# Clamps moved from right in front of two copies, a reordered rounding and 11 fewer filler products in the opening of an attention-plus-MLP kernel

## The chip, the cores and the metric

One core of a Trainium2 chip (trn2). The metric is device microseconds of one execution; lower is better. PE is TensorE, DVE is VectorE, ACT is ScalarE, SP issues the transfers. "Mean clock" is the mean granted clock of TensorE over one execution, as a share of full speed. PSUM is the memory that the kernel's products are written to, in banks (`ps` in the code).

## The reference

```python
def _attn_ref(x, state):                      # B,H,S,Ns,D = 8,8,512,32,64
    scores = matmul(x, state.T) / sqrt(D);  a = softmax(scores);    xread = matmul(a, state)
    scores2 = matmul(state, x.T) / sqrt(D); a2 = softmax(scores2);  sread = matmul(a2, x)
    return concatenate([xread, sread], axis=2)
def _moe_ref(x, w_in, w_out):                 # 4352 tokens, 512 -> 2048 -> 512
    h = x @ w_in
    g = h * (1 / (1 + exp(-1.702 * h)))
    return (g @ w_out).astype(float32)
```

(Shortened to its arithmetic.) The weights arrive as 64-bit floats. They are read as pairs of 32-bit words and rounded to fp32 on the chip: that is the "rounding" of this document. There are 16 pieces of w_in (128 x 512 each, numbered from 0) and 16 of w_out.

## The kernel before

The kernel multiplies state and w_in first: M(b, c) is batch b's state times column block c of w_in, and needs pieces 4c to 4c+3. The up-projection `up_x(b, f)` then multiplies M by the attention weights aT(b). Every M leaves PSUM through a ScalarE copy, and every up-projection block through a gelu on ScalarE. Rounding a piece takes one VectorE mask (it cuts the exponent bits out), two ScalarE clamps (they keep the exponent in range) and four VectorE steps. Batch 0's four blocks go by while batch 1's attention weights are being normalised on VectorE (`att_x_norm`).

```python
def round_a(i):
    ...
    # the two clamps of a piece of w_in, the second reads the first's result
    nc.scalar.activation(out=sc.bitcast(FP32), in_=sc, func=AF.Relu, bias=edge[0], scale=-8.0)     # L200
    nc.scalar.activation(out=sc, in_=sc.bitcast(FP32), func=AF.Relu, bias=edge[1], scale=-1.0)     # L201

def round_b(i):
    ...
    nc.vector.tensor_scalar(fr, hi, 0xFFFFF, 0x100000, ALU.bitwise_and, ALU.bitwise_or)            # L210 fraction
    nc.vector.scalar_tensor_tensor(sc, hi, -0x80000000, sc, ALU.bitwise_and, ALU.bitwise_or)       # L211 sign
    nc.vector.scalar_tensor_tensor(dst, lo, 2.0**-32, fr, ALU.mult, ALU.add)                       # L212 sum
    nc.vector.scalar_tensor_tensor(dst, dst, 2.0**-20, sc.bitcast(FP32), ALU.mult, ALU.mult)       # L213 product

def att_M(b, c, spare=False):
    ps = [psH.tile(...) if spare else att_ps(...) for g in range(NG)]
    by_state(b, ps, lambda rows, j: w_in[c][rows, j])         # quarter j reads piece 4c+j
    for g in range(NG):
        nc.scalar.copy(m[:, g], ps[g])                        # L418

# the opening, from batch 1's scores on
att_scores(1)
keep_warm(14)                 # products of zeros
powers_to(4)
round_to(NPR, 2)              # piece 3; masks and clamps two pieces ahead
att_M(0, 0)
att_blocks(1); att_x_exp(1)
up_x(0, 0); up_x(0, 1); up_x(0, 2, True); up_x(0, 3, True)
round_to(NPR + 1)             # piece 4, with masks and clamps of pieces 6 and 7
att_x_norm(1)
att_M(1, 0)
turn(1, 0, None, [1, 1])      # four up_x(1, .), a rounding after each of the first two
round_to(2 * NPR)             # piece 7, with the clamps of piece 10
att_M(0, 1)
turn(0, 1, (1, 1), [1, 1, 1])
...
```

## Time and profile before

| | before |
|---|---|
| median of the first 3 runs | 744.18 us (743.77 to 744.27) |
| span of the profiled run, mean clock | 742.8 us, 0.998 |
| PE busy | 728.4 us, 98% |
| PE still between M(1,0) and its first product | 2.12 us |
| PE still between M(0,1) and its first product | 1.50 us |

The page's busy shares and the chain are shown in the prediction. The timeline of PE says the same from PE's side; columns are start us, length us, engine, line, operation, output and inputs, count, and in brackets how long the engine stood still before it and who ended that:

```profile
38.01 1.84 PE L289 MATMUL M<-w_in,stT 64*32 64x512 f32 x16
41.97 7.13 PE L458 MATMUL h<-low,M 128*128 128x512 f32 x16 [2.12 <-ACT M L418]
49.04 1.09 PE L289 MATMUL M<-w_in,stT 64*32 64x512 f32 x16
51.63 5.42 PE L458 MATMUL h<-aT,M 128*128 128x512 f32 x12 [1.50 <-ACT M L418]
```

M(1,0) takes 1.84 us instead of 1.09: its second bank is freed only by the newest gelu, which ends at 38.72, and the other products start at 38.77. Then PE stands still twice for a ScalarE copy.

### The profile page before, as it was taken

What the parts mean: (1) busy time and instruction counts of PE and PEld (TensorE: products, weight loads), DVE (VectorE), ACT (ScalarE), POOL (GpSimd) and SP (SyncE); (2) the same over time, 40 slices, a digit from 0 to 9 for tenths busy, and PEclk for the clock granted to TensorE, in tenths of its full rate; (3) what the DMA queues carried; (4) which work ended last, traced back from release to release, by engine and by line L of the source; (5) the groups of instructions that cost most, each with busy time, mean ns of one, the idle gap of its engine ahead of it and who ended that gap; (6) DMA issues with size and microseconds to landing.
All of it is one profiled execution on the core that took longest, in us unless ns stands there. A gap on an engine that the chain in (4) does not pass through costs nothing.

```text
span 742.8 us, 11102 instructions
## 1 busy us (share of the span) xinstructions
PE 728.4 (98%) x4624; PEld 567.7 (76%) x4626; DVE 510.9 (69%) x982; ACT 232.4 (31%) x424; POOL 0.8 (0%) x8
## 2 busy tenths in 40 slices
PE   8989999999999999999999999999999999999996
PEld 3423454467898788888888789878987988899995
DVE  6999799819856776567747776687566774767340
ACT  4676611024214511533133422451143313300220
POOL 0000000000000000000000000000000000000000
PEclk9999999999999999999999999999999999999999
DMA  8921246010031000300040004000130001000000
GB/s 221 351 67 50 84 155 161 0 44 15 15 86 19 1 15 29 75 1 15 1 103 1 15 1 99 6 8 8 36 69 1 15 10 35 1 15 30 15 1 28
DMA packets 48770, 35.31 MB, mean 48 GB/s; under 512 B 36432, under 2 KB 44112, under 8 KB 48720
## 3 DMA queue, kind: packets, MB, share of 16 engines
q1 hardware_dynamic: 48720, 34.61, 16.3%
q8 instruction: 36, 0.59, 0.3%
q14 instruction: 14, 0.11, 0.0%
HBM read 25.69 MB, written 8.91 MB: 47 GB/s over the span
## 4 chain that ended last, share of the span: by engine, by line
PE 96%; DMA 2%; ACT 1%; SPq 0%; issue 0%; DVE 0%; DVEq 0%; ACTq 0%
PE o L642 33%; PE o L887 16%; PE h L458 8%; PE o L476 7%; PE low L594 7%; PE upx L887 6%; PE o L594 5%; PE M L289 4%; PE o L519 2%; PE xT L268 2%; PE warm L122 1%; PE o L289 1%; PE sr L438 1%; PE upx_sr L887 1%; DMA out_dram<-osb_sr 1%; PE eT L427 1%
## 5 line engine op out<-in xcount | busy, mean ns | idle before, releaser
L642 PE MATMUL o<-w_out,g 128*128 128x256 f32 x672 | 151.8, 380 | 0.0
L897 DVE TENSOR_TENSOR g<-o,g 128x512 f32<-128x512 f32 (+1 forms) x140 | 88.1, 651 | 88.4 <-PE o L887 87.4
L642 PEld LDWEIGHTS o<-w_out,g 128*128 128x128 f32 x672 | 125.2, 190 | 21.7 <-issue 5.5
L894 ACT ACTIVATE g<-g 128x512 f32<-128x512 f32 (+1 forms) x84 | 49.8, 599 | 100.5 <-DVE g L897 100.5
L642 PE MATMUL o<-sums,g 128*128 128x256 f32 x224 | 51.1, 382 | 0.0
L642 PE MATMUL o<-sums,later 128*128 128x256 f32 x224 | 49.5, 379 | 0.0
L887 PE MATMUL upx<-aT,M 128*128 128x256 f32 x192 | 49.3, 379 | 0.0
L642 PEld LDWEIGHTS o<-sums,g 128*128 128x128 f32 x224 | 41.5, 190 | 10.1 <-issue 5.0
L887 PE MATMUL o<-ta,M 128*128 128x256 f32 x192 | 49.3, 379 | 0.0
L887 PE MATMUL o<-ta,ms 128*128 128x256 f32 x192 | 48.3, 379 | 0.0
L642 PEld LDWEIGHTS o<-sums,later 128*128 128x128 f32 x224 | 42.6, 190 | 5.8
L418 ACT COPY M<-M 128x512 f32<-128x512 f32 x64 | 33.2, 596 | 38.7 <-PE M L289 38.7
L887 PEld LDWEIGHTS o<-ta,ms 128*128 128x128 f32 x192 | 36.5, 190 | 5.0
L887 PEld LDWEIGHTS upx<-aT,M 128*128 128x128 f32 x192 | 36.5, 190 | 5.0
L887 PEld LDWEIGHTS o<-ta,M 128*128 128x128 f32 x192 | 36.5, 190 | 5.0
L597 DVE TENSOR_TENSOR pu<-low,pu 128x128 f32<-128x128 f32 x14 | 4.1, 290 | 43.5 <-PE low L594 43.5
L499 DVE TENSOR_TENSOR later<-g,g 128x512 f32<-128x512 f32 (+1 forms) x32 | 20.8, 650 | 19.1 <-ACT g L461 19.1
L289 PE MATMUL M<-w_in,stT 64*32 64x512 f32 x512 | 33.2, 594 | 0.2 <-ACT eT L428 0.2
L458 PE MATMUL h<-low,M 128*128 128x512 f32 x64 | 29.8, 600 | 2.1 <-ACT M L418 2.1
L458 PE MATMUL h<-aT,M 128*128 128x512 f32 x64 | 28.7, 599 | 2.3 <-ACT M L418 2.3
L476 PE MATMUL o<-w_out,g 128*128 128x512 f32 x64 | 28.7, 594 | 0.0
L476 PE MATMUL o<-w_out,sums 128*128 128x512 f32 x64 | 28.4, 594 | 0.0
(176 smaller groups left out, 1102.6 us busy)
## 6 DMA issues: line engine op xcount, KB each, us to landing
later<-in_moe_w_out_dram SPq DMA_DIRECT2D x16, 512.0 KB
xn<-in_x_dram SPq DMA_DIRECT2D x28, 256.0 KB
w_out<-in_moe_w_in_dram SPq DMA_DIRECT2D x12, 512.0 KB
out_dram<-osb SPq DMA_DIRECT2D x18, 256.0 KB
out_dram<-later SPq DMA_DIRECT2D x14, 256.0 KB
later<-in_moe_w_in_dram SPq DMA_DIRECT2D x4, 512.0 KB
sums<-in_x_dram SPq DMA_DIRECT2D x4, 256.0 KB
stn<-in_state_dram SPq DMA_DIRECT2D x16, 32.0 KB
```

The lines of the kernel that those rows point to most:

```text
L268: nc.tensor.transpose(ps[:, c], x_heads(b, c, j), ident)
L289: nc.tensor.matmul(ps[g][st], A[b]["stT"][rows, st], rhs(rows, j), start=True, stop=True)
L418: nc.scalar.copy(m[:, g], ps[g])
L458: nc.tensor.matmul(hps, lhs[i], rhs[i], start=(i == 0), stop=(i == n - 1))
L476: nc.tensor.matmul(ops, G[key, f // 2][:, f % 2, P * r : P * (r + 1)], w_out[:, f], start=(f == 0), stop=(f == NF - 1))
L499: nc.vector.tensor_tensor(out=s1, in0=a21, in1=a22, op=ALU.add)
L519: nc.tensor.matmul(ps[:, r], lhs[f][:, P * r : P * (r + 1)], rhs[:, f], start=(first and r == 0 and f == 0), stop=(f == HF - 1), skip_grou ...
L594: nc.tensor.matmul(ps, lhs[f], rhs[:, f], start=(f == 0), stop=(f == QF - 1))
L642: nc.tensor.matmul(ps[:, r], lhs[f][:, P * r : P * (r + 1)], rhs[:, f], start=(r == 0 and f == 0), stop=(f == HF - 1), skip_group_check=True,)
L887: nc.tensor.matmul(ps[:, k], lhs[i][:, o : o + P], rhs[i], start=(first and k == 0 and i == 0), stop=(i == n - 1), skip_group_check=True,)
L894: nc.scalar.activation(out=dst, in_=src, func=AF.Gelu_apprx_sigmoid)
L897: nc.vector.tensor_tensor(out=dst, in0=ps, in1=x, op=ALU.add)
```

## The change

Its intent: let nothing but gelus stand right in front of the copies of M(1,0) and M(0,1) on ScalarE's queue, give M(1,0) banks that are free already, put another step between a rounding step and the one that uses its result where there is one to put, and issue 3 products of zeros where 14 were. The clamps of pieces 6 and 7 move behind the copy of M(1,0). Those of piece 10 stay ahead of the copy of M(0,1), but move from behind the fourth gelu of M(1,0) to before it.

```diff
-    def round_b(i):
+    def fraction(i):
...
+        nc.vector.tensor_scalar(dst.bitcast(I32), words(i)[1], 0xFFFFF, 0x100000, ALU.bitwise_and, ALU.bitwise_or)
+        begun[i] = dst
+    def round_b(i, ahead, follows):
...
+        if i not in begun:
+            fraction(i)
...
-        nc.vector.tensor_scalar(fr, hi, 0xFFFFF, 0x100000, ALU.bitwise_and, ALU.bitwise_or)
         nc.vector.scalar_tensor_tensor(sc, hi, -0x80000000, sc, ALU.bitwise_and, ALU.bitwise_or)
-        nc.vector.scalar_tensor_tensor(dst, lo, 2.0**-32, fr, ALU.mult, ALU.add)
+        powers_to(ahead)
+        nc.vector.scalar_tensor_tensor(dst, lo, 2.0**-32, dst.bitcast(I32), ALU.mult, ALU.add)
...
+        if follows and i + 1 in raw:
+            fraction(i + 1)
         nc.vector.scalar_tensor_tensor(dst, dst, 2.0**-20, sc.bitcast(FP32), ALU.mult, ALU.mult)
...
+    powers_to(1)
+    fraction(0)
     powers_to(2)
     round_to(2, 0)
...
-    keep_warm(14)
+    keep_warm(3)
     powers_to(4)
-    round_to(NPR, 2)
+    round_to(NPR, 1)
     att_M(0, 0)
+    powers_to(NPR + 2)
...
+    att_M(1, 0, True)
     round_to(NPR + 1)
     att_x_norm(1)
-    att_M(1, 0)
...
-    turn(1, 0, None, [1, 1])
-    round_to(2 * NPR)
+    turn(1, 0, None, [1, 1, 1])
     att_M(0, 1)
```

More of the change, by code (lines that the diff above doesn't have):

```diff
@@ L148 @@
     PIECES = [("i", c, k) for c in range(NFC) for k in range(NPR)] + [("o", f) for f in range(NF)]
-    raw, power = {}, {}
+    raw, power, begun = {}, {}, {}
     AHEAD = 3
@@ L201, in round_a @@
         nc.scalar.activation(out=sc, in_=sc.bitcast(FP32), func=AF.Relu, bias=edge[1], scale=-1.0)
-    def round_b(i):
+    def fraction(i):
         key = PIECES[i]
         dst = w_in[key[1]][:, key[2]] if key[0] == "i" else w_out[:, key[1]]
-        fr = dst.bitcast(I32)
+        nc.vector.tensor_scalar(dst.bitcast(I32), words(i)[1], 0xFFFFF, 0x100000, ALU.bitwise_and, ALU.bitwise_or)
[3 more added lines that the diff above has]
+            fraction(i)
+        dst = begun.pop(i)
         lo, hi = words(i)
         sc = power.pop(i)
-        nc.vector.tensor_scalar(fr, hi, 0xFFFFF, 0x100000, ALU.bitwise_and, ALU.bitwise_or)
         nc.vector.scalar_tensor_tensor(sc, hi, -0x80000000, sc, ALU.bitwise_and, ALU.bitwise_or)
-        nc.vector.scalar_tensor_tensor(dst, lo, 2.0**-32, fr, ALU.mult, ALU.add)
+        powers_to(ahead)
+        nc.vector.scalar_tensor_tensor(dst, lo, 2.0**-32, dst.bitcast(I32), ALU.mult, ALU.add)
+        del raw[i]
+        if follows and i + 1 in raw:
+            fraction(i + 1)
         nc.vector.scalar_tensor_tensor(dst, dst, 2.0**-20, sc.bitcast(FP32), ALU.mult, ALU.mult)
-        del raw[i]
     done = {"load": 0, "a": 0, "b": 0, "credit": 0.0}
@@ L234, in round_to @@
     def round_to(n, ahead=AHEAD):
+        nin = NFC * NPR
         while done["b"] < min(n, len(PIECES)):
-            powers_to(min(done["b"] + 1 + ahead, max(NFC * NPR, done["b"] + 1)))
-            round_b(done["b"])
+            i = done["b"]
+            powers_to(i + 1)
+            round_b(i, min(i + 1 + ahead, max(nin, i + 1)), i + 1 < nin and (i + 1 < n or i >= NPR))
             done["b"] += 1
```

## The prediction

> **What bounds the kernel now.** I read the page's busy shares first, then the chain of work that ended last for 0 to 240 us, then VectorE's and ScalarE's timelines for 0 to 75 us, where the diff's lines stand.
>
> ```profile
> PE 728.4 (98%) x4624; PEld 567.7 (76%) x4626; DVE 510.9 (69%) x982; ACT 232.4 (31%) x424; POOL 0.8 (0%) x8
> ```
>
> TensorE is busy for 98% of a 742.8 us span and the chain is 96% PE. A change that adds and removes no product of the result can win only where PE runs filler (the products of zeros, "warm") or stands still. The diff touches nothing after about 75 us except the order of VectorE's work, so the whole prize lies in the first 52 us. The chain of waits there (columns: start us, length us, what):
>
> ```profile
> 26.42 2.75 PE warm L122 x12
> 29.17 1.16 PE M L289 x16
> 30.33 0.57 ACT M L418
> ...
> 30.95 7.15 PE h L458 x16
> ...
> 38.12 0.60 ACT g L461
> 38.72 0.62 ACT low L200
> ...
> 39.36 0.72 ACT low L201
> 40.08 0.62 ACT low L200
> ...
> 40.73 0.72 ACT low L201
> 41.45 0.48 ACT M L418
> ...
> 41.97 7.15 PE h L458 x16
> ...
> 49.74 0.62 ACT low L200
> ...
> 50.38 0.72 ACT low L201
> 51.11 0.48 ACT M L418
> ...
> 51.63 5.42 PE h L458 x12
> ```
>
> Three things are to be seen. M(0,0) starts at 29.17, exactly where the warm products end: 14 of them fill 26.05 to 29.17, or 0.223 us each. M(1,0) goes to PE at 38.10, but its copy (line 418) starts on ScalarE only after four clamps (lines 200 and 201, those of pieces 6 and 7), and the next real product comes at 41.97. M(0,1) meets the same at 49.1: one pair of clamps (piece 10) stands ahead of its copy, and PE restarts at 51.63. From 51.63 on the chain is PE without a gap worth naming, until two copies of 0.6 us at 87 and 99.8 us that the diff leaves alone.
>
> VectorE's timeline (start, length, engine, line, operation) gives the rounding:
>
> ```profile
> 25.13 0.44 DVE L210 TENSOR_SCALAR w_in<-w_out 128x512 int32<-128x512 int32 x1
> 25.47 0.70 DVE L211 SCALAR_TENSOR_TENSOR low<-w_out,low 128x512 int32<-128x512 int32 x1
> 26.07 0.70 DVE L212 SCALAR_TENSOR_TENSOR w_in<-w_out,w_in 128x512 f32<-128x512 uint32 x1
> 26.81 0.69 DVE L213 SCALAR_TENSOR_TENSOR w_in<-w_in,low 128x512 f32<-128x512 f32 x1
> 27.41 1.31 DVE L320 STREAM_TRANSPOSE e<-o 128x512 f32<-128x512 f32 x2
> ...
> 37.21 1.25 DVE L370 STREAM_TRANSPOSE low<-e 128x1024 f32<-128x1024 f32 x1
> ```
>
> Piece 3, the last that M(0,0) needs, is done at 27.50, so even now M(0,0) waits 1.6 us for filler alone. Line 370 ends at 38.46: it writes the normalised weights of batch 1, without which the products after M(1,0) cannot start. That is a second floor close under ScalarE's.
>
> **What the Trainium skill says.** "ScalarE: Activation LUTs", section "What ACT_TABLE_LOAD costs", gives an ACTIVATE with a pointer bias as about 280 ns + 0.833 ns per column, 706 ns for 512, and says that back-to-back ones overlap by about 93 ns. The trace agrees: 706 to 716 ns for line 200, and 0.63 us from a line-201 start to the next line-200 start. Line 201 reads what line 200 wrote and starts 0.75 us after it, with no overlap. "VectorE: DVE Perf Modes", section "The DRAIN you can't avoid", says that the next operation waits until the pipe is empty. Here it depends on the data: line 212 starts 0.60 us after the 0.70 us line 211, whose result it does not use; line 213 starts 0.74 us after line 212, whose result it does use. So a use of the predecessor's result costs some 0.12 us. "TensorE: Matmul & The Clock Gate", section "Part 1: The HAM clock gate", says that an idle window of about 3.4 us halves the clock; the longest stillness of PE in this stretch is 2.12 us and the granted clock is 0.998. The change shortens those gaps, so I expect no cold product from cutting the filler.
>
> **The change part by part.** Start-to-start steps from the trace: fraction or mask 0.34 us, each three-operand step 0.61, plus 0.11 to 0.13 where a step uses its predecessor's result.
>
> *Front, to 26 us.* Rounding of pieces 0 and 1 starts 2 us earlier for one fraction and ends at about 11.5 instead of 11.95, but VectorE next waits for PE at 12.26 and PE waits for x from memory. Worth 0.
>
> *Fewer products of zeros.* In the old order a mask of piece 5 waited 0.5 us for its transfer ahead of piece 3's rounding. In the new one VectorE, free at 23.89, does fraction 23.89, sign 24.23, mask of piece 4 at 24.84, sum 25.18, product 25.91 (0.73 later, this one still uses its predecessor), done at 26.6. PE: scores end at 26.05, 3 fillers with the 0.05 issue end at 26.7 to 26.9. The two nearly tie; I take 26.8. M(0,0) moves from 29.17 to 26.8: **2.37 us**. Its copy needs ScalarE at 27.94, where the clamps of piece 4 end at about 26.7. Products of M(0,0) then start at 26.8 + 1.78 (30.95 less 29.17) = 28.58.
>
> *M(1,0)'s copy ahead of four clamps.* PE is through four blocks at 28.58 + 7.15 = 35.73 and goes to M(1,0). It now has the other pair of banks, so it need not wait for the newest gelus (in the old trace that stretches M(1,0) to 1.84 us). The copy starts at 35.73 + 1.14 = 36.87, and by it alone products could start at 37.51. But VectorE: mask of piece 5 at 26.52, blocks 26.86, maximum 28.21, subtraction 29.46, fraction 4 at 30.60, sign 30.94, two masks to 32.22, sum, fraction 5, product at 33.17, then sum of exponentials 33.78 and the same chain of 1.24 + 0.22 + 0.39 + 1.25 us to the transpose at 36.88, which ends at 38.13. Products of M(1,0) start at 38.17, VectorE setting it. From M(1,0) to there is 2.44 us instead of 3.87: **1.43 us**.
>
> *M(0,1)'s copy ahead of clamps.* ScalarE, through M(1,0)'s copies at 37.83, now does the postponed clamps of pieces 6 and 7 (2.74 us as before) until 40.57, then three units of a gelu and two clamps (0.49 + 0.75 + 0.63 = 1.86 us), the fourth gelu at 46.16, and the copy of M(0,1) at 46.65 with nothing between. Products follow 0.62 us after the copy's start, as before: 47.27. PE would be at M(0,1) at 38.17 + 7.15 = 45.32 and done at 46.34, so ScalarE is 0.3 us behind it. Start to start 9.10 instead of 9.66 us: **0.56 us**. Piece 7, by VectorE's new cycle of 2.51 us (old 2.73), is done at about 45.7; M(0,1) uses it only in its last quarter, so that fits barely.
>
> *After that.* Everything from 51.63 moves as a block to 47.27. VectorE gains less (piece 15 done at about 64.5 instead of 67.2), but M(0,3), which needs it, comes at about 69, and VectorE stands still 5.14 us for ScalarE's exponentials near 79 as it is. The shorter cycle of the later roundings is therefore worth nothing by itself there. Sum: 2.37 + 1.43 + 0.56 = 4.36 us; 744.18 - 4.36 = 739.8, or 0.6% less.
>
> **The rivals.** First, the floor under M(1,0): if VectorE's order gains nothing (dependent or not), its normalisation ends near 38.5 and the second part shrinks by 0.4, but ScalarE's backlog sets 47.27 anyway: 739.8 to 740.2. Second, clamps postponed are not removed: if ScalarE's backlog of 2.74 us runs on, gelus come late, PE waits for banks, and M(0,1) keeps its old delay: the third part becomes 0 or -1 us, 740.4 to 741.4. For it: ScalarE is solid from 37 to 47 us by my sum, its 1.86 us unit is longer than PE's 1.79 us block. Against it: it idled 1.59 and 0.86 us in the same stage before. Third, piece 3 or piece 7 late on VectorE makes PE wait where filler stood: 0.3 to 1 us lost. Fourth, the gain is given back before 83 us because VectorE's rounding or a transfer becomes the bound: 741 to 744; against it, the first product at 83.14 needs a piece finished at 73.9. Fifth, a better outcome, if normalisation ends before the copy: up to 0.6 us more at the second part, but ScalarE's backlog swallows it.
>
> **Range and chances.** The predicted time is 739.8 us. Run to run the kernel before spreads 0.5 us; the three terms are uncertain by about 0.2, 0.4 and 0.6 us, more to the slow side: 738.9 to 741.2 in 8 of 10. A gain over 2% would need 14.9 us, more than all of PE's stillness and filler in this stage after 26 us; a loss over 2% has no source. So faster 0.01, same 0.98, slower 0.01.
>
> **What would show it.** In the changed profile: M(0,0) on PE at 26.8; the first product of M(1,0) at about 38.2, released by VectorE's transpose of line 370's kind and not by a copy; the clamps of pieces 6 and 7 after the copy of M(1,0); the first product of M(0,1) at about 47.3 behind ScalarE; PE solid from there, the chain's later entries all about 4.4 us earlier. It is wrong if M(0,0) starts later than 27.2 (piece 3 is late), if PE shows a new wait for a bank between 38 and 47 us, or if the shift at the first down product (83.14 before) is less than at 47.

## The result, and the profile after

The changed kernel took 739.31 us (median of 4 runs, 739.24 to 739.40); beside it the kernel before took 744.22 us (median of 4, 743.77 to 745.60). The ratio is 0.9931, 95% interval 0.9914 to 0.9948: "same" at the 2% mark, and the gain is real. A ratio is the mean time of one kernel's runs over the mean of the other's of the same rounds, so not quite the ratio of the medians.

The chain of waits of the changed kernel (start us, length us, what; lines are shifted by 13 against before: 471 for 458, 302 for 289, 431 for 418, 474 for 461):

```profile
25.83 0.38 PE warm L122
26.21 1.16 PE M L302 x16
...
27.98 7.13 PE h L471 x16
35.11 1.13 PE M L302 x16
36.24 1.05 ACT M L431 x2
37.30 0.63 ACT low L200
...
45.59 0.48 ACT g L474
46.07 0.53 ACT M L431
...
46.65 5.42 PE h L471 x12
```

M(0,0) follows 3 fillers. The copy of M(1,0) stands directly behind M(1,0). From there the chain runs through ScalarE alone, five pairs of clamps and four gelus, to the copy of M(0,1). PE's timeline has the other two limits of the stage:

```profile
37.59 7.10 PE L471 MATMUL h<-low,M 128*128 128x512 f32 x16 [1.46 <-DVE low L383]
44.62 1.35 PE L302 MATMUL M<-w_in,stT 64*32 64x512 f32 x16
46.65 5.42 PE L471 MATMUL h<-aT,M 128*128 128x512 f32 x12 [0.67 <-ACT M L431]
```

The first product of M(1,0) waits for VectorE's last step of the normalisation (line 383), no longer for a copy. M(0,1) takes 1.35 us instead of 1.09: VectorE ends piece 7 at 44.87, and the four products that read it end 1.1 us after that. And the product behind it waits for ScalarE. Without any wait M(0,1) would have ended at 45.71; piece 7 puts that to 45.97, and ScalarE is through its gelus at 46.07. Three limits lie within 0.4 us.

| stretch, PE's view of the chain | before | after | gain |
|---|---|---|---|
| end of batch 1's scores to start of M(0,0) | 26.05 to 29.17 = 3.12 | 25.45 to 26.21 = 0.76 | 2.36 |
| to the first product of M(1,0) | 12.80 | 11.38 | 1.42 |
| to the first product of M(0,1) | 9.66 | 9.06 | 0.60 |
| to the first down-projection product | 31.51 | 31.50 | 0.01 |
| sum | | | 4.39 |

The two profiled spans differ by 742.8 - 737.6 = 5.2 us. Of the rest, 0.60 us lies ahead of all this: x arrived sooner, so the scores ended at 25.45 instead of 26.05. The experiments say what that is. The last 0.25 us lies far behind the change, where ScalarE waits for an output tile to be stored before it refills it. Before, then after:

```profile
165.64 0.58 ACT L483 COPY osb<-o 128x512 f32<-128x512 f32 x1 [3.83 <-DMA out_dram<-osb]
158.95 0.58 ACT L496 COPY osb<-o 128x512 f32<-128x512 f32 x1 [2.13 <-PE xT L281]
```

In five of the fourteen profiles (both of the kernel before, and those of a_warm14, b_order and b_copies, which are told of below) the third store of this group takes 2.48 to 2.82 us, and the one 16 KB packet of the instruction queue falls into it. In the other nine that packet falls elsewhere, the store takes 1.17 to 1.43 us, and nothing is lost. The five lose 0.2 to 0.6 us by it near 189 us. This meeting of two transfers is read from the traces; no run tests it.

### The profile page after: what moved, and what is told of

Read it like the earlier page. It is cut to its first block, busy times and chain, and to the rows that moved or that the text cites. A ratio compares the mean times of both kernels' runs of the same rounds, so it can differ in the third digit from the quotient of the medians.

```text
span 737.6 us, 11080 instructions
## 1 busy us (share of the span) xinstructions
PE 724.4 (98%) x4613; PEld 566.4 (77%) x4615; DVE 509.7 (69%) x982; ACT 232.3 (31%) x424; POOL 0.8 (0%) x8
## 4 chain that ended last, share of the span: by engine, by line
PE 95%; ACT 2%; DMA 2%; SPq 0%; DVE 0%; issue 0%; DVEq 0%; ACTq 0%
PE o L655 33%; PE o L900 16%; PE o L489 8%; PE low L607 7%; PE h L471 7%; PE upx L900 6%; PE o L607 5%; PE M L302 4%; PE o L532 2%; PE xT L281 2%; PE o L302 1%; PE sr L451 1%; PE warm L122 1%; PE upx_sr L900 1%; DMA out_dram<-osb_sr 1%; PE eT L440 1%
## 5 line engine op out<-in xcount | busy, mean ns | idle before, releaser
L614 ACT COPY pu<-o 128x128 f32<-128x128 f32 x14 | 3.7, 265 | 80.0 <-PE o L607 60.0
```

## The experiments

Kernels named a_ are the changed kernel with one thing undone, b_ the kernel before with one part alone, c_ are attempts to go further. All gave correct results. In the traces I compare the stretch from the start of M(0,0) to the first product of M(0,1): 22.46 us before, 20.44 after. It is free of the arrival of x.

### 14 fillers again

```diff
-    keep_warm(3)
+    keep_warm(14)
```

> The changed kernel with 14 products of zeros again in place of 3, all else as changed. My theory: M(0,0) starts 11 x 0.215 = 2.36 us later (about 28.6 us if the front is that of the changed profile), ScalarE's solid stretch from the copy of M(1,0) on moves with it, and the whole delay reaches the end: 739.3 + 2.3 = 741.6 us (741.2 to 742.0). Rival: VectorE, which does not move with the filler, is the real bound in the stage behind it, so that part of the delay is absorbed there: 739.3 to 740.5 us.

Measured 741.87 us (741.63 to 742.24, 4 runs), 2.56 more than the changed kernel. M(0,0) starts at 28.53 instead of 26.21, and the first product of M(0,1) at 48.92 instead of 46.65, 2.27 later. So the filler's time goes through to the end in full (the rest of the 2.56 us is the late store told of above). VectorE absorbed part of it at the first product of M(1,0), which comes 1.59 us later (39.18 instead of 37.59), but not at M(0,1), where ScalarE's queue sets the time.

### M(1,0) late again

```diff
-    att_M(1, 0, True)
     round_to(NPR + 1)
     att_x_norm(1)
+    att_M(1, 0)
```

> The changed kernel with M(1,0) put back behind the rounding of piece 4 (four clamps ahead of its copy on ScalarE, the old pair of banks). My theory: the copy starts near 38.4 us instead of 36.2, the first product of M(1,0) near 39.0 instead of 37.6, but ScalarE then has no backlog at M(0,1), so about 1.2 us reaches the end: 740.5 us (740.2 to 740.9). Rival, that postponed clamps only move the wait (the copies' place is worth nothing): 739.3 us within 0.2.

Measured 741.36 us (740.67, 740.89, 741.82, 742.57). From M(0,0) at 26.25 to the first product of M(0,1) at 47.96 are 21.71 us: 1.27 us more, as expected. The run takes back the place and the banks of M(1,0) together; none separates them. The faster two runs agree with that (1.4 to 1.6 us over the changed kernel). The slower two do not; the one at 742.57 has a mean clock of 0.997, the others 0.999 to 1.0. More on this below. PE's old 2.12 us of stillness is back:

```profile
35.09 1.84 PE L302 MATMUL M<-w_in,stT 64*32 64x512 f32 x16
39.05 7.13 PE L471 MATMUL h<-low,M 128*128 128x512 f32 x16 [2.12 <-ACT M L431]
```

### M(0,1) behind clamps again

```diff
-    turn(1, 0, None, [1, 1, 1])
+    turn(1, 0, None, [1, 1])
+    round_to(2 * NPR)
```

> The changed kernel with the clamps of piece 10 ahead of M(0,1)'s copy again. My theory: the fourth gelu then waits for PE to 44.8 us and the clamps behind it put the copy at about 46.65 instead of 46.0: + 0.65 us, 739.95 us (739.7 to 740.2). Rival, that ScalarE's backlog is the same in either order: 739.3 us.

Measured 739.94 us (739.84 to 740.12), 0.63 more; the first product of M(0,1) is at 47.34, 0.69 later with a front that is 0.1 later. As expected.

### The old order inside a rounding

The old `round_b` with its masks first, in the changed kernel's places; the front of pieces 0 and 1 as before.

> The changed kernel with the old order inside a rounding (masks first, then the four steps one after another, no fraction of the next piece in between; also the old front for pieces 0 and 1). My theory: VectorE's order is worth little; piece 7 comes some 1 us later, and M(0,1) waits for it in its last quarter: + 0.2 to 0.3 us, 739.55 us (739.3 to 739.9). Rival, that the reordering earns most of the gain: 740.8 us or more. Front: if the 0.6 us by which x arrived sooner in the changed profile was only a difference from run to run, it may be seen with this old front too; if the earlier fraction brought it, the first transpose of x is back at 9.0 us and the time near 740.1.

Measured 739.83 us (739.75 to 740.31), 0.52 more, at the upper side of what I expected. The reordering is worth half a microsecond, and here is where: M(0,1) now waits longer for piece 7.

```profile
44.38 1.96 PE L292 MATMUL M<-w_in,stT 64*32 64x512 f32 x16
```

Against 1.35 us in the changed kernel and 1.09 without any wait. VectorE ends piece 7 at 45.24 here, and M(0,1) ends at 46.34; in the changed kernel it was 44.87 and 45.97. Both times M(0,1) ends 1.10 us after its last piece. The first transpose of x stood at 8.28 us, earlier than in any profile so far, with the old front. So the earlier fraction is not what brought x sooner.

### The kernel before once more

> The kernel before, unchanged, as a control of the front. In its first profile the first transpose of x stood at 8.99 us, in the five profiles of the changed family at 8.28 to 8.54, and its time spread over 2.5 us in the last rounds (743.69 to 746.18). If that is the x transfer's difference from run to run, this profile may show another value anywhere in 8.2 to 9.5 and its times spread again (743.5 to 746.5); if something in the program makes x late, it stands at 9.0 again. From the first M product to the first product of M(0,1) I expect 22.46 us as before in either case.

Measured 744.33, 743.90, 745.58, 745.63, 744.28 and 745.76 us. In its profile the first transpose of x stood at 8.42 us (8.99 in its first profile, 8.40 in the changed kernel's), with an unchanged program. The 0.60 us at the front is therefore a difference from run to run, not part of the change. The stretch from M(0,0) at 28.57 to the first product of M(0,1) at 51.03 is 22.46 us again. (Its span is only 0.25 us shorter all the same, because it loses 0.60 us by the late store where the first profile loses 0.25.) But its times fall into two groups: three at 743.9 to 744.3 with a mean clock of 0.998, three at 745.6 to 745.8 with 0.996.

### Only the new order of a rounding

The kernel before with the new `fraction`, `round_b` and `round_to`, and the early fraction of piece 0.

> The kernel before with only the new order inside a rounding and the early fraction of piece 0; 14 fillers and the old places of the copies. My theory: M(0,0) waits for filler and the copies for clamps, so the order is worth nothing here: the stretch from M(0,0) to the first product of M(0,1) stays 22.4 us within 0.3, the time is that of the kernel before within 0.3 us (if the front is alike). Rival, that the order by itself earns much of the gain: at least 2 us less.

Measured 745.59 us (744.29 to 746.01), ratio 1.0002 (0.9988 to 1.0017): nothing by itself. Four of five runs have a mean clock of 0.996 or 0.997, and this profile fell on one of them. PE's timeline and then the clock by stretch (start:end us, length, busy time and count of each engine, granted clock, share of DMA, GB/s):

```profile
41.33 8.83 PE L471 MATMUL h<-low,M 128*128 128x512 f32 x16 [2.12 <-ACT M L431]
```

```profile
41.33:42.50 1.17, 1.17 (x3) 0.68 (x4) 1.17 (x4) 0.43 (x1) 0.00 (x0) 1.00 0.00 0
42.50:44.00 1.50, 1.50 (x3) 0.67 (x2) 1.50 (x4) 0.09 (x1) 0.00 (x0) 0.54 0.05 11
44.00:45.50 1.50, 1.50 (x3) 0.47 (x3) 0.80 (x2) 1.47 (x3) 0.00 (x0) 0.50 0.00 0
```

The same stretch of the second profile of the kernel before, a run at 0.998:

```profile
42.50:44.00 1.50, 1.50 (x4) 0.60 (x4) 1.47 (x5) 0.60 (x2) 0.00 (x0) 1.00 0.00 0
44.00:45.50 1.50, 1.50 (x5) 0.73 (x4) 1.43 (x4) 1.47 (x3) 0.00 (x0) 1.00 0.00 0
```

Sixteen products that take 7.13 us elsewhere took 8.83 here, because TensorE's clock fell to half 1.28 us after the end of the 2.12 us gap. The trace's clock record has it at 0.5 for 3.413 us. That explains the two groups of times, as far as one profile of a slow-clock run can. Take those 1.70 us off, and the stretch from M(0,0) at 28.53 to the first product of M(0,1) at 52.68, 24.15 us, is 22.45: unchanged by the order.

### Only the filler

```diff
-    keep_warm(14)
+    keep_warm(3)
```

> The kernel before with 3 products of zeros in place of 14, nothing else. My theory: M(0,0) is then held by piece 3, done 2.1 us before the point where it began before minus the mask's wait, so it starts 1.6 us sooner (27.55 with the old front), not 2.4; the stage behind moves with it because the copies wait for clamps that follow the gelus: 1.6 us less (1.3 to 1.9). Rival: VectorE's normalisation, which does not move, holds the first product of M(1,0), and 0.5 us or less is left. Second rival: fewer fillers let the clock fall, and products of the stage behind get longer than 0.43 us of PE each.

Measured 743.04 us: 741.97 and 742.07 at a clock of 0.998 and 0.999, and 743.12, 743.65 and 743.04 at 0.996 and 0.997. The profile is one of the first kind. M(0,0) starts at 26.26, at once behind the 3 fillers and not at 27.55 as I wrote: its first three quarters need only pieces 0 to 2. It then waits for piece 3 in its last quarter and lasts 1.70 us instead of 1.16. It ends at 27.96 instead of 29.73, and the first product of M(0,1) comes at 49.27 instead of 51.03: 1.76 us, close to the 1.6 expected. What this leaves of the changed kernel's 2.36 us is 0.6 us, which took moving the mask of piece 5, with its wait for a transfer, behind the rounding of piece 3: a_oldbody, with the old order inside a rounding but the new places, has M(0,0) at its full speed (1.09 us).

### Only the copies

```diff
-    round_to(NPR + 1)
-    att_x_norm(1)
-    att_M(1, 0)
+    att_M(1, 0, True)
+    round_to(NPR + 1)
+    att_x_norm(1)
...
-    turn(1, 0, None, [1, 1])
-    round_to(2 * NPR)
+    turn(1, 0, None, [1, 1, 1])
```

> The kernel before with only the two copies of M ahead of the clamps (M(1,0) in the other pair of banks), 14 fillers and the old order. My theory: from M(0,0) at 29.17 the copy of M(1,0) is at 39.2, the first product at 39.9 instead of 41.97, ScalarE's backlog sets the copy of M(0,1) at 49.0 and its first product at 49.6 instead of 51.63: 2.0 us less (1.7 to 2.3). Rival, postponed clamps give it all back: within 0.4 us of the kernel before.

Measured 741.90 us (741.77 to 742.44). From M(0,0) at 28.71 to the first product of M(0,1) at 49.10 are 20.39 us, 2.07 less than before, as expected. And none of its five runs is a slow-clock one (0.998 to 1.0).

### Filler in the gap

The new theory: PE's 2.12 us of stillness lets the clock fall in some executions. It is tested by filling the gap, in the kernel before.

```diff
     att_x_norm(1)
     att_M(1, 0)
+    keep_warm(8)
```

> The kernel before with 8 more products of zeros behind M(1,0), in the 2.12 us in which PE stands still there. New theory (from the earlier runs): some executions of every kernel with that 2.12 us gap ran about 1.7 us longer at a mean clock of 0.996 or 0.997, and the one profile of such a run shows half clock for 3.4 us right behind the gap; the gap lets the clock fall. Then the filler (8 x 0.215 = 1.7 us, fits in the gap) takes the slow executions away and costs nothing: all runs within 743.6 to 744.6 us, none at 745.4 or above, where about half of the kernel before's are. Rival: the clock's fall has nothing to do with that gap: about half of these runs again lie at 745.4 to 746.2.

Measured 743.73, 743.71, 743.77, 744.78 and 743.78 us, all at a mean clock of 0.998 or more. Of the eight runs of the kernel before in the same rounds, five were at 745.4 to 745.8 with 0.996 or 0.997. The filler hides in the gap, which is now 0.29 us, and the products behind stay where they were:

```profile
39.37 1.67 PE L122 MATMUL warm<-sums 128*128 128x512 bf16 x7 [0.16 <-issue]
41.33 1.98 PE L458 MATMUL h<-low,M 128*128 128x512 f32 x4 [0.29 <-ACT M L418]
```

The run at 744.78 lies a little outside what I expected, but its clock did not fall; it is unexplained, like the 741.82 above. Counted over all runs whose clock was listed, "slow-clock" meaning 0.996 or 0.997 and over 1 us above the kernel's fastest (the mean clock alone does not tell: every profile also ends with 2.71 to 5.70 us at half clock, after the last product):

| kernels | PE still behind M(1,0) | slow-clock runs |
|---|---|---|
| before (with its control) | 2.12 us | 14 of 22 |
| b_order, b_warm3, a_m10_late | 2.12 us | 4 of 5, 3 of 5, 1 of 4 |
| b_gapfill | 0.29 us | 0 of 5 |
| the changed kernel and all others | 0.73 to 1.46 us | 0 of 36 |

For the kernel before, the mean of the 14 is 745.66 us and of the other 8 it is 744.23: 1.4 us.

Why does the clock fall in only some executions with the same gap? The clock records of the traces show it. In all 14 traces the clock changes only at marks 3.413 us apart (the stretches at full clock last 11, 204, 214 or 215 times that), and the first mark lies anywhere from 3.90 to 7.17 us after the start. Cut each trace into windows at these marks, and sum how long PE stood still in each. The 15 windows that end in a fall (14 behind the last product, and the one of b_order) hold 2.12 us of stillness or more. The other 2986 windows at full clock hold 1.83 us or less. In the profiles with the 2.12 us gap the window with most of it holds:

| profile | PE still in one window | clock falls |
|---|---|---|
| before, before_again, a_m10_late, b_warm3 | 1.52, 1.69, 1.74, 1.83 us | no |
| b_order | 2.12 us, the whole gap | yes |

So a gap of 2.12 us matters when a window takes in nearly all of it, and by these figures one of 1.46 us does not. By my estimate from these figures a random position of the marks gives a fall in 38% to 55% of executions; 22 of 36 is 61%. No run was made to test this.

### Going further: the normalisation first

```diff
-    round_to(NPR + 1)
-    att_x_norm(1)
+    att_x_norm(1)
+    round_to(NPR + 1)
```

> The changed kernel with batch 1's normalisation on VectorE ahead of the rounding of piece 4, so that it ends near 35.5 us instead of 37.4 and the first product of M(1,0) waits only for its copy (36.85 instead of 37.6). My theory that ScalarE's backlog sets the first product of M(0,1): nothing is gained, 739.3 us within 0.2. Rival that VectorE's normalisation is the bound of the stage: 0.7 us less, 738.6 us.

Both theories missed. Measured 740.61 us (740.50 to 741.86), 1.3 us slower than the changed kernel. VectorE, put on the normalisation first, has to stand still for ScalarE's exponentials, and everything behind it, up to piece 7, comes later. VectorE's timeline shows the loss and PE's shows who pays:

```profile
31.18 1.22 DVE L378 TENSOR_REDUCE sm<-e 128x32 f32<-128x1024 f32 x1 [1.12 <-ACT e L371]
```

```profile
36.89 7.55 PE L471 MATMUL h<-low,M 128*128 128x512 f32 x16 [0.73 <-ACT M L431]
44.37 1.08 PE L302 MATMUL M<-w_in,stT 64*32 64x512 f32 x12
46.19 1.05 PE L302 MATMUL M<-w_in,stT 64*32 64x512 f32 x4 [0.74 <-DVE w_in L225]
```

The first product of M(1,0) does come 0.7 us sooner. But the last four products of M(0,1) wait for piece 7 (line 225) until 46.19. They then last 1.05 us, about as long as the twelve before them (1.08) or all sixteen together (1.09): the quarters run side by side, and a late one costs nearly the whole time of an M. So the first product of M(0,1) comes at 47.90 instead of 46.65. In the changed kernel the rounding of piece 4 fills the time in which the exponentials run.

### Going further: both, and fewer ahead

c_both also does the clamps of piece 6 ahead of the fourth gelu of M(0,0); c_best also drops the filler ahead of M(0,0) and lets masks and clamps run two pieces ahead instead of three.

```diff
     up_x(0, 2, True)
+    powers_to(NPR + 3)
     up_x(0, 3, True)
```

> As c_norm_first, and the clamps of piece 6 done ahead of the fourth gelu of M(0,0), where ScalarE idles 1.1 us. If ScalarE's backlog of four clamps and VectorE's normalisation together are the bound, the copy of M(0,1) starts at about 45.15 us (PE and piece 7 set it) instead of 46.0: 0.85 us less, 738.45 us (738.1 to 738.8). If something else holds PE there, within 0.2 us of 739.3.

> As c_both, with no filler ahead of M(0,0) (its last quarter then waits for piece 3) and masks and clamps one piece less ahead (two instead of three). M(0,0) starts at 25.5 us and ends at 26.6 instead of 27.4; piece 7 is done at 44.4 and sets M(0,1)'s last quarter; first product of M(0,1) near 45.4 instead of 46.65: 1.2 us less than the changed kernel, 738.1 us (737.7 to 738.6). If clamps come too late for VectorE with one piece less ahead, 738.5 to 739.5.

Measured 740.27 us (740.12 to 740.95) and 739.88 us (739.84 to 740.06). Both keep VectorE's wait for the exponentials of c_norm_first (0.79 us is left as stillness, a mask fills the rest) and with it the wait for piece 7: M(0,1)'s last quarter starts at 45.67 and 45.42. My expectations had worked out piece 7 for both as if VectorE lost nothing. In c_best M(0,0) starts at 24.51, but its last quarter waits for piece 3 to 25.97, so most of the filler's removal is lost too. No version beat the changed kernel.

## Why the prediction was right or wrong

The time was right: 739.8 us predicted, 739.31 measured, inside 738.9 to 741.2, and "same" at the 2% mark. The measured gain, 744.22 - 739.31 = 4.91 us, is 0.5 us above the sum of the terms, 4.36. The 8 undisturbed later runs of the kernel before (mean 744.23) say the same. The late store, 0.25 and 0.60 us in the two profiles of the kernel before and not in the changed kernel's, is of that size; the prediction did not foresee it.

*The three terms* were right one by one. Fewer products of zeros: 2.37 us predicted, 2.36 in the table of stretches. M(1,0): 1.43 and 1.42, and set by VectorE's transpose as written. M(0,1): 0.56 and 0.60, set by ScalarE. Undoing the first in the changed kernel costs 2.27 us at the first product of M(0,1); undoing the copies' places one at a time costs 1.27 and about 0.6.

*The front, worth 0,* was right. The 0.60 us by which the changed kernel's profile was ahead there comes and goes in the kernel before itself (8.99 and 8.42 us).

*After 51.63 everything moves as a block* was right: 31.51 and 31.50 us to the first down-projection product.

*The reordering worth little* was right for the kernel before (ratio 1.0002), but in the changed kernel it is worth 0.52 us. The prediction wrote that M(0,1) uses piece 7 "only in its last quarter, so that fits barely", and gave the order no number of its own. The last quarter alone lasts 1.05 us, so M(0,1) ends 1.10 us after piece 7 whenever that comes after its start; it did not fit, and M(0,1) took 1.35 us. By the prediction's own 45.7 us for piece 7, M(0,1) would have ended at 46.8, behind the 46.65 that it gives for the copy. The third term came out near its 0.56 us in part by luck: VectorE was some 0.2 us earlier than written, once the 0.6 us of the front is taken off. Since ScalarE's backlog and piece 7 end together, each hides part of the other.

*Wrong was the reading of the clock in the kernel before.* The step was: the clock halves after an idle window of about 3.4 us, "the longest stillness of PE in this stretch is 2.12 us and the granted clock is 0.998", so no cold product. For the changed kernel that held. For the kernel before, from which the forecast counts, it was read from one profile, which had fallen on an undisturbed execution, and so had the three runs from which a spread of 0.5 us was taken (its later 22 runs go from 743.69 to 746.18). In 14 of 22 listed runs the same 2.12 us gap went with a mean clock of 0.996 or 0.997, and one profile of a kernel with that gap shows half clock for 3.4 us and 1.70 us more for the same 16 products. The change shortens the gap to 1.46 us, and no such run was seen among 36 runs of the kernels with the shorter gap. So the change gains 4.4 us in the stretches that it touches, about half a microsecond where the kernel before meets the late store, and some 1.4 us more in executions where the clock would have fallen. This fits the changed kernel's four runs, within 0.16 us, and the kernel before's band of 2.5. The sum of 4.36 us fits the comparison with b_gapfill, whose profile has neither a clock fall in the gap nor the late store: 743.77 - 739.31 = 4.46 us.

*The fifth rival* (an earlier normalisation is swallowed by ScalarE's backlog) was not borne out in the way tried here: done by order alone, the earlier normalisation costs 1.3 us, because VectorE then stands still and piece 7, not ScalarE's backlog, holds M(0,1).

What stays open: whether the windows of the clock record are the whole reason for the falls, whether the late store depends on the change's earlier times or on chance, and single runs about 1 us long at full clock (744.78, 741.86, 741.82).

## What to carry to other kernels

Look for the operation that the bound engine waits for, and for what stands ahead of it on its engine's queue without being needed yet (here four clamps, 2.74 us); but count what the postponed work does next, here a ScalarE backlog that set the following copy. When three limits lie within 0.4 us, as here, moving one earlier at the cost of another can lose time (1.3 us in c_norm_first). And look at the spread and the mean clock of many runs before calling a gap harmless: one profile can show the lucky execution.

## What the Trainium skill lacked or had wrong

- "TensorE: Matmul & The Clock Gate", "Why this matters for your kernels", says "No PE-idle gaps >~3µs between matmul bursts". Taken alone, that lets pass a gap of 2.12 us, which here went with slow-clock runs in 22 of 36 executions; with 1.46 us or less there were 0 of 41. In the traces every window with 2.12 us of stillness or more was followed by a fall, and none with 1.83 us or less. The fall in b_order lasted 3.413 us, which agrees with the window of 3413 ns in the page's "Part 1: The HAM clock gate", and cost 1.70 us.
- "VectorE: DVE Perf Modes", "The DRAIN you can't avoid", says that the next operation does not start until the pipe is empty, and adds that one which is not held starts earlier. It gives no figure for a use of the predecessor's result. In these traces a step that does not use it starts 0.60 us after the start of a 0.70 us step, one that does use it 0.71 to 0.74 us after. The reordering that this allows was worth 0.52 us in the changed kernel.
- "ScalarE: Activation LUTs", "What ACT_TABLE_LOAD costs", fits (706 to 725 ns for line 200 against 706), but gives no figure for two dependent ACTIVATEs: they do not overlap here (0.75 us from start to start for a 0.72 us one, 0.63 where independent).
- The same page and section add a drain of about 1.38 us to a table load of 1.28 us. The load of 1.28 us is in the changed kernel's trace (31.13 us), but no drain: the exponentials ahead of it end at 31.11 and the gelu behind it starts at 32.42.
